# Attention's row maxima sent by GpSimd, score products emitted slot by slot, prologue loads sooner

## The chip, the cores and the metric

The program runs on one core of a Trainium2 chip. The number is the device time of one execution in microseconds (us): 728.79 us is the median of the kernel before, from two runs at 728.57 and 729.01 us. Engines are named as the profile names them: PE is TensorE (PEld its weight loads, PEq its sequencer), DVE is VectorE, ACT is ScalarE, POOL is GpSimd, SP is SyncE. [...]

## The reference

Two independent parts are computed and laid side by side in the last axis.

```python
# A: attention with memory.  S=2048, D=576, 32 heads of 18 channels, 4 segments of L=512
q,k,v = heads(x@wq), heads(x@wk), heads(x@wv)      # (1, 32, 4, 512, 18) each
M = 0; z = 0
for s in range(4):
    p = softmax(q[s] @ k[s].T * 18**-0.5 + causal_mask)     # 512 x 512 per head
    a_dot = p @ v[s]
    a_mem = (phi(q[s]) @ M) / (phi(q[s]) @ z + 1e-6)
    outs[s] = g*a_mem + (1-g)*a_dot                          # g = sigmoid(beta)
    M += phi(k[s]).T @ v[s];  z += sum(phi(k[s]))
a = concat(outs) @ wo
# B: spectral filter
b = irfft2(rfft2(x_B) * (w_r + 1j*w_i))
```

The softmax takes off the largest score of each row before the exponential. It is these row maxima that the change is about.

## The kernel before

**The stages.** By the profiled execution the forward transform of B takes the first 65 us. From there to about 265 us the projections of A run (q, k, v and the products for M). The inverse transform of B, sixteen steps `u` that PE bounds, lies between 280 and 349 us, and the prologue of the attention is laid between its steps. Attention runs from 351 to 682 us, and the last segment's output projection ends the program at 724 us. The text below is on the attention and its prologue.

**Stacks and row halves.** The 32 heads of 4 segments are 128 units of work, grouped in 16 stacks `n` of eight heads of one segment. A stack of Q (`s.Qs[n%3]`) and one of K (`s.Ks[n%4]`) stand in SBUF with four heads on partitions 0 to 63 (row half R=0) and four on partitions 64 to 127 (R=1). In each half 54 rows hold a head's 18 channels in bf16 parts. Q's rows 54 and 55 hold the row maxima in two bf16 parts, and K's same rows hold -1, so that a product over 56 rows is a score less its row's maximum. The first Q and K stack lie with the mask in one tile named `x0`, which the profile prints as `x`; the others are printed as `Qs` and `Ks`. A Q or K stack is loaded by four DMAs of `stack_dmas`, two of 384 KB and two small ones, which SP issues.

**One unit k.** There are 32 units `k`, two to a stack (`n,qd=divmod(k,2)`). For each, in this order:

1. `fill` (L689): products of 54 rows with one half's heads into a PSUM tile `s1`, of which there are three; then DVE takes the largest of each row into `mg` (L693). There are ten fills to a unit, of the kinds A, B and C, with sixteen reductions.
2. `mpath` (L701 to L710): POOL splits `mg` into two bf16 parts, `mh` (L701, L702); PE transposes them into PSUM, `mt` (L705); ACT copies that into SBUF, `mts` (L708); and two DMAs of 4 KB (`send`, L710) carry `mts` into rows 54 and 55 of the two halves of Q.
3. `s2` (L720 through `scores`): ten score tiles of 512 columns, each as a first pass (b=0, 56 rows, with the maxima) and a second pass (b=1, 54 rows) over a PSUM tile `s2`, of which there are four; then ACT takes the exponential into `P` (L729).
4. POOL puts zeros above the diagonal (`sel`, L743), four selects to a unit, two at once and two (`rest`) one step later.
5. `pv` (L766) multiplies P with V, ACT copies the result to `U` (L772), and DMAs carry U away.

**What sets the order.** `attention` is a loop of 133 steps `t`, with k=t//4 and hh=t%4. Each engine runs its instructions in the order in which it gets them. A step pops loads off the list `q` onto SP (three at t%8==0, else one), then emits `seg(t)`, a quarter of unit k's `s2` with fills of unit k+2 or k+3 between them, then background work, a part of `pv` of unit k-1, a part of `mpath`, and `rest`; last come the calls that `later` put off (`due`). `later(2,...)` runs a call two steps on. A fill, and so the maximum, of a unit is ready some steps ahead of its `s2`:

- hh=2 of unit k: `mpath(k+2)` starts on POOL;
- hh=3 of unit k: `mt` on PE, `mts` on ACT;
- hh=0 of unit k+1: the send, behind the step's two exponentials on ACT;
- hh=0 of unit k+2: the first `s2` that needs the rows.

The four loads of each of the stacks Qs(n+2) and Ks(n+3) come off the list from t%8==0 on.

**The prologue.** Units 0 and 1 and a part of unit 2 get their fills while the inverse runs: 15 steps with one or two fills each, two of 21 load calls popped in each step. The inverse yields several times for each `u`; one prologue step is taken at every fourth yield (`i%4==1`) beyond the seventh, and what is left is emitted behind the inverse. Here `send` goes to POOL (`s.now<0`), 4 DMAs in all; the other 60 go to ACT.

Of the kernel before, what the change touches and what calls it, by code (L numbers as in the profile page):

```python
# [6 lines left out]
AF=mybir.ActivationFunctionType; OP=mybir.AluOpType  # L7
# [95 lines left out]
class FFT:  # L103
# [4 lines left out]
    def forward(s,xp,cp,pp,wl,xs,consts):  # L108
# [301 lines left out]
class ATT:  # L410
# [284 lines left out]
    def mpath(s,k):  # L695

        nc=s.nc; n,qd=divmod(k,2); Q=s.Qs[n%3]
        mh=s.mh.rearrange("p a m -> p (a m)"); mg=s.mg.pop(k).rearrange("p (r h) i -> p r (h i)",r=2)
        hi,lo=[mh[:,:32].rearrange("p (r a m) -> p r a m",r=2,a=2)[:,:,a] for a in range(2)]
        e=nc.vector if s.now>=115 else nc.gpsimd  # L700
        e.tensor_copy(hi,mg)  # L701
        e.tensor_tensor(lo,mg,hi,op=OP.subtract)  # L702
        yield
        pt=s.psm.tile([128,1024],BF,name="mt",tag=s.mtag)[:,:128]
        nc.tensor.transpose(pt,mh,s.idb)  # L705
        yield
        mt=s.sm.tile([32,128],BF,name="mts",bufs=2)
        nc.scalar.copy(mt,pt[:32])  # L708
        def send(eng):
            for R in range(2): eng.dma_start(Q[64*R+54:64*R+56,0,2*qd:2*qd+2].rearrange("p h (i c) -> p (h i) c",c=128),mt[16*R:16*R+16])  # L710
        if s.now<0: send(nc.gpsimd)
        else: s.later(2,lambda: send(nc.scalar))
        yield
    def scores(s,p,n,J):

        Q,K=s.Qs[n%3],s.Ks[n%4]; f=True
        for b,rows in ((0,56),(1,54)):
            for i,(o,h,kb,qo) in enumerate(J):
                R,j=h//4,h%4; r=slice(64*R,64*R+rows)
                s.nc.tensor.matmul(p[:,o:o+512-qo],K[r,1-b,j,128*kb:128*kb+128],Q[r,b,j,qo:],start=f,stop=b==1,skip_group_check=True)  # L720
                f=False
    def s2(s,k,kind,x):
        nc=s.nc; n,qd=divmod(k,2); h=2*qd+(4*x if kind==2 else 4*(x//2)+x%2); tp=s.tp
        if k not in s.P: s.P[k]=[tp.tile([128,4,w],F32,name=f"P{i}") for i,w in enumerate((512,512,256))]
        P=s.P[k]
        p=s.ps.tile([128,512],F32,name="s2",tag="s2")
        J={0:[(0,h,0,0)],1:[(0,h,1,128),(384,h,3,384)],2:[(0,h,2,256),(256,h+1,2,256)]}[kind]
        s.scores(p,n,J)
        nc.scalar.activation(P[2][:,2*x:2*x+2].rearrange("p h c -> p (h c)") if kind==2 else P[kind][:,x],p,AF.Exp,scale=SC)  # L729
    def seg(s,t):  # L730

        k,q=divmod(t,4)
        L=(((0,0),("C",3),(0,2),("A",1)),((1,0),(1,2),("C",1),(2,1),("B",1),("B",0)),
           ((0,1),("A",2),(0,3),("C",0)),((1,1),(1,3),("A",3),(2,0),("C",2),("A",0)))[q]
        for a,x in L:
            if a in (0,1,2):
                if k<32: s.s2(k,a,x)
            elif k+2+q//2<32: s.fill(k+2+q//2,a,x)
        if k>31 or q%2==0: return
        P=s.P[k]  # L740
        def sel(x,a=0,b=1):
            x=x[:,a::b]
            s.nc.gpsimd.affine_select(out=x,in_=x,pattern=[[0,4//b],[1,128]],compare_op=OP.is_ge,fill=0.0,base=0,channel_multiplier=-1)  # L743
# [212 lines left out]
    def prologue(s):  # L956

        nc,io=s.nc,s.io
        yield
        s.load_v(0)  # L960
        q=s.stack_dmas(1,0)+s.stack_dmas(1,1)+s.stack_dmas(2,0)+s.stack_dmas(2,1)+[lambda: s.load_v(1)]+s.stack_dmas(3,1)
        for i in range(2): yield
        i=0; m=None
        O=((("C",3),("A",1)),(("C",1),("B",1)),(("B",0),)); E=((("A",2),("C",0)),(("A",3),("A",0)),(("C",2),))
        for k,F in ((0,E),(0,O),(1,E),(1,O),(2,E)):
            for f in F:
                for a,x in f: s.fill(k,a,x)
# [147 lines left out]
def emit(nc,tc,io):  # L1115
    def pool(es,name,bufs=1,**kw):
        return es.enter_context(tc.tile_pool(name=name,bufs=bufs,reuse_waits="tile",**kw))
    with ExitStack() as L0:
        cp=pool(L0,"cp"); dp=pool(L0,"dp",space=bass.MemoryType.DRAM)
        A=ATT(nc,tc,io,cp,dp)  # L1120
        Rz=ExitStack(); Rv=ExitStack(); Rw=ExitStack(); Ri=ExitStack(); L1x=ExitStack()
        tc.swap_default_side()
        zp=pool(Rz,"z"); ftp=pool(Rz,"ft")
        wq=pool(Rw,"wq")
        tc.swap_default_side()
        A.wh,A.wl={},{}
        F=FFT(nc,tc,io,zp); F.tp=A.ftp=ftp
        with tc.manual_schedule():
            x0=pool(L1x,"x0")
            with ExitStack() as es:  # L1130
                xp=pool(es,"xf",2); cf=pool(es,"cf"); st=pool(es,"st",2)
                pf=es.enter_context(PP(tc,"pf",dict(f1=2,c1=2)))
                F.forward(xp,cf,pf,A.load_w("wqk",1152,wq,st,576,"wst",4,1),A.first(Slots(x0),xp),A.consts)
            with ExitStack() as es:
                wv=pool(Rv,"wv"); xp=pool(es,"xp"); tp=pool(es,"tp",2); fwp=pool(es,"fw",2)
                pp=es.enter_context(PP(tc,"pp",dict(pj=5,pt=1,pm=2)))
                F.pace.add(F.middle(fwp)); F.pace.add(F.last())
                def hook(g,i):
# [12 lines left out]
                q0=[]  # L1151
                A.projections(xp,tp,pp,wv,F.pace,hook)
            Rv.close()
            with ExitStack() as L1:
                cp2=pool(L1,"cp2"); sm=pool(L1,"sm",2); sp=pool(L1,"sp",3)
                ps1=L1.enter_context(PP(tc,"ps1",dict(s1=3)))
                A.begin(sm,sp,ps1)
                with ExitStack() as es:
                    pi=es.enter_context(PP(tc,"pi",dict(i2=2,i3=2,mt=1)))
                    yl=pool(es,"yl",2)  # L1160
                    A.att_setup(cp2)
                    A.psm,A.mtag=pi,"mt"
# [27 lines left out]
```

## Time and profile before

| | us |
|---|---|
| median of 2 runs | 728.79 (728.57 to 729.01) |
| the profiled execution | 725.92 |
| its span | 724.2 |
| PE busy | 682.5 (94% of the span) |
| PE weight loads | 490.1 (68%) |
| DVE busy | 543.0 (75%) |
| ACT busy | 432.7 (60%) |
| POOL busy | 191.2 (26%) |
| mean granted PE clock | 0.978 of full speed |

The span is the time from the first to the last recorded instruction, and the execution is 1.7 us longer. "Busy" leaves out the time in which an engine issues DMAs. In a row of a timeline stand the start, the time that one takes, the engine, the line, the operation, out<-in, the shape, and in brackets how long the engine had stood idle and whom it waited for. In a row of waits stand the idle time, the number of waits and the longest or mean of them. A row of a table by windows has the length of the window, the busy time and number of instructions of PE, PEld, DVE, ACT and POOL, the granted clock, the share of the 16 DMA engines, and GB/s. In the DMA view, q1 is the queue of what SP issues, q10 that of ACT, and q0 that of POOL: packets, MB, and the share of the 16 engines' time.

### The profile page before, as it was taken

Reading aid. Unit: us, or ns where it says so; the run is one execution under the profiler, and the core shown is the slowest. Engines: PE = TensorE matmul, PEld = TensorE weight load, DVE = VectorE, ACT = ScalarE, POOL = GpSimd, SP = SyncE. Lnnn points to the kernel's source line nnn. Section 1 sums busy time; section 2 is a strip of 40 time slices with the busy share of each in tenths; the row PEclk is TensorE's granted clock in tenths of the full one; section 3 lists DMA queues with packets and bytes.
Section 4 is the critical chain, followed back from the end, with each engine's and each line's share of the span. In section 5 each row is a group of like instructions: output and inputs, shape, how many; then the busy total and the mean of one; then the engine's idle time right before and its main releaser. Section 6 shows DMA issues by size and latency. Waiting matters only on the chain.

```text
span 724.2 us, 15284 instructions
## 1 busy us (share of the span) xinstructions
PE 682.5 (94%) x5288; PEld 490.1 (68%) x5288; DVE 543.0 (75%) x1514; ACT 432.7 (60%) x900; POOL 191.2 (26%) x389
## 2 busy tenths in 40 slices
PE   9999999999999999999888798879999999899997
PEld 6999789789789799999534344434566445563496
DVE  5998988888898786777876776768656877468633
ACT  4876783873782844443476656648656676466421
POOL 2112000100100114572253322334323463133300
PEclk9999999999999999999898989999999999999999
DMA  9995665783685796998378865766766786333052
GB/s 344 301 286 140 191 184 161 249 267 107 208 264 135 220 287 185 247 248 193 108 147 166 173 142 118 187 164 130 163 122 172 188 173 132 77 118 92 24 168 71
DMA packets 79748, 127.66 MB, mean 176 GB/s; under 512 B 13052, under 2 KB 44442, under 8 KB 79542
## 3 DMA queue, kind: packets, MB, share of 16 engines
q1 hardware_dynamic: 72766, 110.67, 58.3%
q0 software_dynamic: 5824, 15.76, 8.0%
q8 instruction: 42, 0.69, 0.4%
q10 hardware_dynamic: 1080, 0.25, 0.2%
q14 instruction: 36, 0.29, 0.1%
HBM read 81.78 MB, written 43.92 MB: 174 GB/s over the span
## 4 chain that ended last, share of the span: by engine, by line
PE 50%; DMA 13%; DVE 7%; ACT 6%; issue 5%; POOL 2%; SPq 1%; ACTq 1%; DVEq 0%; POOLq 0%
PE pj L487 10%; PE pv L766 7%; DMA Qs<-mts 6%; PE pjv L487 6%; PE s L720 6%; PE i L331 4%; PE i L320 4%; DVE junk L693 4%; PE po L912 4%; PE s L689 3%; ACT P L729 2%; DMA x<-mts 2%; PE po L942 2%; PE pm L559 2%; DMA vD<-vt 1%
## 5 line engine op out<-in xcount | busy, mean ns | idle before, releaser
L693 DVE CUSTOM_DVE_ANT_0 junk<-s,x 128x384 bf16<-128x384 f32 (+3 forms) x512 | 218.4, 487 | 84.3 <-PE s L720 55.8
L729 ACT ACTIVATE P<-s 128x512 f32<-128x512 f32 x320 | 168.0, 605 | 54.9 <-PE s L720 33.0
L743 POOL TENSOR_SCALAR_AFFINE_SELECT P<-P 128x512 f32<-128x512 f32 (+1 forms) x131 | 78.9, 626 | 51.0 <-ACT P L729 50.3
L720 PEld LDWEIGHTS <-Ks 56*128 56x128 bf16 (+1 forms) x768 | 48.3, 96 | 52.6 <-issue 25.0
L766 PE MATMUL pv<-P,vs 128*32 128x512 f32 (+3 forms) x1024 | 81.9, 452 | 0.0
L720 PE MATMUL s<-Qs,Ks 56*128 56x512 bf16 (+7 forms) x512 | 66.9, 307 | 9.7 <-DMA Qs<-mts 7.1
L689 PE MATMUL s<-Ks,Qs 54*128 54x384 bf16 (+3 forms) x256 | 58.2, 309 | 5.1 <-DVE mg L693 5.1
L766 PEld LDWEIGHTS pv<-P,vs 128*32 128x32 f32 x1024 | 28.7, 112 | 50.1 <-issue 41.1
L487 PE MATMUL pj<-x,wqkh 128*128 128x512 f32 x162 | 56.1, 408 | 0.0
L232 DVE TENSOR_TENSOR Z<-Z 128x580 f32<-128x580 f32 (+2 forms) x51 | 45.9, 913 | 0.6
L693 DVE DVE_READ_ACCUMULATOR2_ANT mg<- 128x1 f32 x512 | 42.6, 83 | 0.0
L689 PEld LDWEIGHTS <-Qs 54*128 54x128 bf16 x320 | 27.2, 96 | 19.5 <-issue 13.6
L548 POOL MEMSET vt<- 128x32 f32 x16 | 2.4, 163 | 139.9 <-PE pm L559 121.6
L720 PE MATMUL s<-x,Ks 56*128 56x128 bf16 (+7 forms) x256 | 33.2, 305 | 5.3 <-DMA x<-mts 5.0
L320 PE MATMUL i<-civ,Y 128*128 128x256 f32 (+1 forms) x288 | 37.1, 282 | 0.9 <-POOL Y L305 0.9
L708 ACT COPY mts<-mt 32x128 bf16<-32x128 bf16 x32 | 8.1, 254 | 49.0 <-PE mt L705 47.3
L320 PEld LDWEIGHTS i<-civ,Y 128*128 128x128 f32 (+1 forms) x288 | 35.3, 180 | 1.3 <-POOL Y L305 1.3
L487 PE MATMUL pj<-x,wqkl 128*128 128x512 f32 x90 | 35.6, 395 | 0.0
L487 PE MATMUL pj<-xh,wqkh 128*128 128x512 f32 x90 | 35.5, 395 | 0.0
L487 PE MATMUL pj<-xh,wqkl 128*128 128x512 f32 x90 | 35.5, 395 | 0.0
L331 PE MATMUL i<-itab,T 128*128 128x290 f32 (+1 forms) x224 | 34.5, 304 | 0.6 <-ACT E L336 0.5
L506 DVE SCALAR_TENSOR_TENSOR ex<-pj,ex 128x512 f32<-128x512 f32 (+1 forms) x28 | 19.3, 690 | 20.7 <-ACT ex L504 20.7
(189 smaller groups left out, 1596.8 us busy)
## 6 DMA issues: line engine op xcount, KB each, us to landing
qkD<-sp SPq DMA_DIRECT2D x32, 384.0 KB
Ks<-qkD SPq DMA_DIRECT2D x24, 384.0 KB
x<-qkD SPq DMA_DIRECT2D x20, 384.0 KB
Qs<-qkD SPq DMA_DIRECT2D x20, 384.0 KB
xin<-xb SPq DMA_DIRECT2D x16, 384.0 KB
cfw<-cfw POOLq DMA_DIRECT2D x16, 384.0 KB, 4.5
civ<-civ POOLq DMA_DIRECT2D x16, 384.0 KB, 6.1
vs<-vD SPq DMA_DIRECT2D x16, 310.5 KB
```

The costliest lines, as they stand in the source:

```text
L232: s.nc.vector.tensor_tensor(o,a,b,op=op)
L320: nc.tensor.matmul(p[:m,k],Y[i][:,q,c*128:c*128+m],cc[:,hl,o:o+256],start=n==0,stop=n==5)
L331: nc.tensor.matmul(p,x,t,start=n==0,stop=n==6)
L487: s.nc.tensor.matmul(out,a,b,start=i==0,stop=i==len(L)-1)
L506: if r1>r0: nc.vector.scalar_tensor_tensor(e[r0:r1],ps[r0:r1],0.0,e[r0:r1],op0=OP.max,op1=OP.add)
L689: nc.tensor.matmul(p[:,o:o+128*i+128],Q[r,0,j,128*i:128*i+128],K[r,1,j,:128*(i+1)],start=True,stop=True)
L693: nc.vector.tensor_tensor_reduce(out=junk[:,:w],in0=p[:,o:o+w],in1=s.mask[:,512-w:],scale=1.0,scalar=-3.0e38, op0=OP.add,op1=OP.max,accum_ ...
L720: s.nc.tensor.matmul(p[:,o:o+512-qo],K[r,1-b,j,128*kb:128*kb+128],Q[r,b,j,qo:],start=f,stop=b==1,skip_group_check=True)
L729: nc.scalar.activation(P[2][:,2*x:2*x+2].rearrange("p h c -> p (h c)") if kind==2 else P[kind][:,x],p,AF.Exp,scale=SC)
L743: s.nc.gpsimd.affine_select(out=x,in_=x,pattern=[[0,4//b],[1,128]],compare_op=OP.is_ge,fill=0.0,base=0,channel_multiplier=-1)
L766: nc.tensor.matmul(s.pvt[32*hh:32*hh+32,128*j:],vt[:,152*j+19*h:152*j+19*h+32],mv[0][:,hh,mv[1]],start=j==0,stop=j>1,skip_group_check=True)
L912: nc.tensor.matmul(ps,a[t][:r,c],b[:r,t,w],start=i==0,stop=i==13)
```

## The change

It has three parts.

1. **The sends.** `send` now goes to POOL in the attention too, and with `later(0)` in place of `later(2)`: in the step of the copy `mts`, not two calls of `due` on. Sixty DMAs move from ACT's queue to POOL's.
2. **The order of the products.** `seg` before emitted a flat list of score tiles and fills. Now each step has two lists, one for each row half, and `s2` is a generator that yields behind each pass. One slot takes one pass or one fill from each list.
3. **The prologue.** Each prologue step pops three load calls, with a yield behind each, and the inverse takes a step at three of four yields (`i%4!=3`).

```diff
@@ mpath
-        def send(eng):
-            for R in range(2): eng.dma_start(Q[64*R+54:64*R+56,0,2*qd:2*qd+2].rearrange("p h (i c) -> p (h i) c",c=128),mt[16*R:16*R+16])
-        if s.now<0: send(nc.gpsimd)
-        else: s.later(2,lambda: send(nc.scalar))
+        def send():
+            for R in range(2): nc.gpsimd.dma_start(Q[64*R+54:64*R+56,0,2*qd:2*qd+2].rearrange("p h (i c) -> p (h i) c",c=128),mt[16*R:16*R+16])
+        if s.now<0: send()
+        else: s.later(0,send)
         yield
-    def scores(s,p,n,J):
-
-        Q,K=s.Qs[n%3],s.Ks[n%4]; f=True
-        for b,rows in ((0,56),(1,54)):
-            for i,(o,h,kb,qo) in enumerate(J):
-                R,j=h//4,h%4; r=slice(64*R,64*R+rows)
-                s.nc.tensor.matmul(p[:,o:o+512-qo],K[r,1-b,j,128*kb:128*kb+128],Q[r,b,j,qo:],start=f,stop=b==1,skip_group_check=True)
-                f=False
     def s2(s,k,kind,x):
...
-        s.scores(p,n,J)
-        nc.scalar.activation(P[2][:,2*x:2*x+2].rearrange("p h c -> p (h c)") if kind==2 else P[kind][:,x],p,AF.Exp,scale=SC)
-    def seg(s,t):
-
-        k,q=divmod(t,4)
-        L=(((0,0),("C",3),(0,2),("A",1)),((1,0),(1,2),("C",1),(2,1),("B",1),("B",0)),
-           ((0,1),("A",2),(0,3),("C",0)),((1,1),(1,3),("A",3),(2,0),("C",2),("A",0)))[q]
+        for b,rows in ((0,56),(1,54)):
+            for i,(o,h,kb,qo) in enumerate(J):
+                R,j=h//4,h%4; r=slice(64*R,64*R+rows)
+                nc.tensor.matmul(p[:,o:o+512-qo],K[r,1-b,j,128*kb:128*kb+128],Q[r,b,j,qo:],start=b==0 and i==0,stop=b==1,skip_group_check=True)
+            if b: nc.scalar.activation(P[2][:,2*x:2*x+2].rearrange("p h c -> p (h c)") if kind==2 else P[kind][:,x],p,AF.Exp,scale=SC)
+            yield
+    def half(s,k,q,L):
+
         for a,x in L:
             if a in (0,1,2):
-                if k<32: s.s2(k,a,x)
-            elif k+2+q//2<32: s.fill(k+2+q//2,a,x)
+                if k<32: yield from s.s2(k,a,x)
+            elif k+2+q//2<32:
+                s.fill(k+2+q//2,a,x)
+                yield
+    def seg(s,t):
+
+        k,q=divmod(t,4)
+        L=((((0,0),("A",1)),(("C",3),(0,2))),(((1,0),("C",1),("B",0)),((1,2),(2,1),("B",1))),
+           (((0,1),("C",0)),(("A",2),(0,3))),(((1,1),(2,0),("A",0)),((1,3),("A",3),("C",2))))[q]
+        for _ in itertools.zip_longest(*[s.half(k,q,l) for l in L]): pass
@@ prologue
                 for a,x in f: s.fill(k,a,x)
-                for _ in range(2):
-                    if q: q.pop(0)()
...
-                yield
+                for _ in range(3):
+                    if q: q.pop(0)()
+                    yield
@@ emit
-                        if i>7 and i%4==1: next(pr,None)
+                        if i>7 and i%4!=3: next(pr,None)
```

The three parts show in the order of the instructions. On ACT, before, at the end of unit 7 and the start of unit 8 (P_5525 and P_5526 are P tiles of unit 8, `Qs_3169` the Q stack into which unit 9's maxima go):

```order
L708 COPY mts<-mt 32x128
L772 COPY U<-pv 128x512
L729 ACTIVATE P_5525<-s_5528 128x512
L729 ACTIVATE P_5525<-s_5536 128x512
L710 DMA Qs_3169<-mts 2x8x128 x2
L729 ACTIVATE P_5526<-s_5552 128x512
```

The sends stand two exponentials behind their copy; in the order of after ACT has no L710 row in the attention. On POOL at the same place, first before, then after (P_5368 to P_5370 are unit 7's P tiles before, P_5370 to P_5372 after; the L701 row is the first of a unit's `mpath`):

```order
L702 TENSOR_TENSOR mh<-mg,mh 128x2x8
L743 AFFINE_SELECT P_5368<-P_5368 128x4x128
L743 AFFINE_SELECT P_5369<-P_5369 128x4x128 x2
L743 AFFINE_SELECT P_5370<-P_5370 128x4x128
L701 CAST mh<-mg 128x2x8
```

```order
L702 TENSOR_TENSOR mh<-mg,mh 128x2x8
L745 AFFINE_SELECT P_5370<-P_5370 128x4x128
L745 AFFINE_SELECT P_5371<-P_5371 128x4x128
L710 DMA Qs_3169<-mts 2x8x128 x2
L745 AFFINE_SELECT P_5371<-P_5371 128x4x128
L745 AFFINE_SELECT P_5372<-P_5372 128x4x128
L701 CAST mh<-mg 128x2x8
```

The sends now stand between a unit's second and third select, so the third and fourth select wait for `mts`, too. On PE, the start of unit 8's first step, first before, then after (s_5528 and s_5536 before, s_5530 and s_5538 after, are its score tiles; s_5532 and s_5540 are fills of unit 10):

```order
L705 MATMUL mt<-idb,mh 128x128
L720 LDWEIGHTS x_2634
L720 MATMUL s_5528<-Qs_3169,x_2634 128x512
L720 LDWEIGHTS x_2634
L720 MATMUL s_5528<-Qs_3169,x_2634 128x512
L689 LDWEIGHTS Qs_3170
L689 MATMUL s_5532<-Ks_3171,Qs_3170 128x512
```

```order
L705 MATMUL mt<-idb,mh 128x128
L724 LDWEIGHTS x_2634
L724 MATMUL s_5530<-Qs_3169,x_2634 128x512
L689 LDWEIGHTS Qs_3170
L689 MATMUL s_5532<-Ks_3171,Qs_3170 128x512
L724 LDWEIGHTS x_2634
L724 MATMUL s_5530<-Qs_3169,x_2634 128x512
```

The fill of the other half now stands between the two passes of the first score tile. On PE at the end of the inverse (L331 is its last product), first before, then after:

```order
L331 MATMUL i_4229<-itab_2955,T_4129 128x290
L689 LDWEIGHTS Qs_3169
L689 MATMUL s_4244<-Ks_3171,Qs_3169 128x384
L689 LDWEIGHTS Qs_3169
L689 MATMUL s_4244<-Ks_3171,Qs_3169 128x128
L689 LDWEIGHTS Qs_3169
L689 MATMUL s_4251<-Ks_3171,Qs_3169 128x512
L705 LDWEIGHTS mh
L705 MATMUL mt<-idb,mh 128x128
```

```order
L331 MATMUL i_4261<-itab_2955,T_4150 128x290
L689 LDWEIGHTS Qs_3169
L689 MATMUL s_4275<-Ks_3171,Qs_3169 128x512
L724 LDWEIGHTS x_2634
L724 MATMUL s_4302<-x_2634 128x512
```

Before, eight fill products, of which the first three are shown, and the transpose of unit 1 stand between the inverse and the first score product; after, one fill product does.

More of the change, by code (lines that the diff above doesn't have):

```diff
@@ L708, in mpath @@
         nc.scalar.copy(mt,pt[:32])
-        def send(eng):
-            for R in range(2): eng.dma_start(Q[64*R+54:64*R+56,0,2*qd:2*qd+2].rearrange("p h (i c) -> p (h i) c",c=128),mt[16*R:16*R+16])
-        if s.now<0: send(nc.gpsimd)
-        else: s.later(2,lambda: send(nc.scalar))
+        def send():
+            for R in range(2): nc.gpsimd.dma_start(Q[64*R+54:64*R+56,0,2*qd:2*qd+2].rearrange("p h (i c) -> p (h i) c",c=128),mt[16*R:16*R+16])
+        if s.now<0: send()
+        else: s.later(0,send)
         yield
-    def scores(s,p,n,J):
-        Q,K=s.Qs[n%3],s.Ks[n%4]; f=True
-        for b,rows in ((0,56),(1,54)):
-            for i,(o,h,kb,qo) in enumerate(J):
-                R,j=h//4,h%4; r=slice(64*R,64*R+rows)
-                s.nc.tensor.matmul(p[:,o:o+512-qo],K[r,1-b,j,128*kb:128*kb+128],Q[r,b,j,qo:],start=f,stop=b==1,skip_group_check=True)
-                f=False
     def s2(s,k,kind,x):
         nc=s.nc; n,qd=divmod(k,2); h=2*qd+(4*x if kind==2 else 4*(x//2)+x%2); tp=s.tp
+        Q,K=s.Qs[n%3],s.Ks[n%4]
         if k not in s.P: s.P[k]=[tp.tile([128,4,w],F32,name=f"P{i}") for i,w in enumerate((512,512,256))]
@@ L727, in s2 @@
         J={0:[(0,h,0,0)],1:[(0,h,1,128),(384,h,3,384)],2:[(0,h,2,256),(256,h+1,2,256)]}[kind]
-        s.scores(p,n,J)
-        nc.scalar.activation(P[2][:,2*x:2*x+2].rearrange("p h c -> p (h c)") if kind==2 else P[kind][:,x],p,AF.Exp,scale=SC)
+        for b,rows in ((0,56),(1,54)):
[5 more added lines that the diff above has]
+    def half(s,k,q,L):
+        for a,x in L:
+            if a in (0,1,2):
+                if k<32: yield from s.s2(k,a,x)
+            elif k+2+q//2<32:
+                s.fill(k+2+q//2,a,x)
+                yield
     def seg(s,t):
         k,q=divmod(t,4)
-        L=(((0,0),("C",3),(0,2),("A",1)),((1,0),(1,2),("C",1),(2,1),("B",1),("B",0)),
-           ((0,1),("A",2),(0,3),("C",0)),((1,1),(1,3),("A",3),(2,0),("C",2),("A",0)))[q]
-        for a,x in L:
-            if a in (0,1,2):
-                if k<32: s.s2(k,a,x)
-            elif k+2+q//2<32: s.fill(k+2+q//2,a,x)
+        L=((((0,0),("A",1)),(("C",3),(0,2))),(((1,0),("C",1),("B",0)),((1,2),(2,1),("B",1))),
+           (((0,1),("C",0)),(("A",2),(0,3))),(((1,1),(2,0),("A",0)),((1,3),("A",3),("C",2))))[q]
+        for _ in itertools.zip_longest(*[s.half(k,q,l) for l in L]): pass
         if k>31 or q%2==0: return
```

## The prediction

> **What bounds the kernel now.** The page first. PE is busy for most of the span and leads the chain of work that ended last, but one DMA stands high in that chain:
>
> ```profile
> span 724.2 us, 15284 instructions
> PE 50%; DMA 13%; DVE 7%; ACT 6%; issue 5%; POOL 2%; SPq 1%; ACTq 1%; DVEq 0%; POOLq 0%
> PE pj L487 10%; PE pv L766 7%; DMA Qs<-mts 6%; PE pjv L487 6%; PE s L720 6%; PE i L331 4%; PE i L320 4%; DVE junk L693 4%; PE po L912 4%; PE s L689 3%; ACT P L729 2%; DMA x<-mts 2%; PE po L942 2%; PE pm L559 2%; DMA vD<-vt 1%
> ```
>
> `Qs<-mts` (6%) and `x<-mts` (2%) are the 4 KB sends. Who waits for them is told by the view of the tile mts over the whole program, and where, by PE's waits from 358 to 474 us:
>
> ```profile
>   PE s L720: 14.3, 6
> PE s L720 <- DMA Qs<-mts: 9.3, 4, 2.4
> PE s L720 <- DMA x<-mts: 5.0, 2, 3.3
> ```
>
> Score products stood still six times for 14.3 us, all in that stretch (9.3 + 5.0). One of them in the timeline, from the copy to the product that waits:
>
> ```profile
> 425.48 1.81 POOL L743 TENSOR_SCALAR_AFFINE_SELECT P<-P 128x512 f32<-128x512 f32 x3 [0.34 <-ACT P L729]
> 426.71 0.26 ACT L708 COPY mts<-mt 32x128 bf16<-32x128 bf16 x1 [0.81 <-PE mt L705]
> 427.53 0.65 ACTq L710 DMA_DIRECT2D Qs<-mts  x1
> 428.22 0.62 ACTq L710 DMA_DIRECT2D Qs<-mts  x1
> 432.77 1.28 PE L766 MATMUL pv<-P,vs 128*32 128x384 f32 x16
> 436.39 0.60 PE L720 MATMUL s<-Qs,x 56*128 56x512 bf16 x1 [2.17 <-DMA Qs<-mts]
> ```
>
> The copy is done at 426.97, ACT issues 0.56 us later, and 8 us on PE still has no maxima. The DMA view of the two stretches says why (queue, packets, MB, share of the 16 engines' time; 427.5 to 434.8 us first, then 434.8 to 436):
>
> ```profile
> q1 hardware_dynamic: 354, 1.21, 96.6%
> ...
> q1 hardware_dynamic: 74, 0.17, 68.3%
> q10 hardware_dynamic: 36, 0.01, 7.2%
> ```
>
> ACT's queue q10 moved no packet for 7.3 us while SP's stack loads filled q1; its 36 packets (two sends) ran when SP's were through. What a stall costs beyond its idle time is seen in windows (length; PE, PEld, DVE, ACT, POOL busy; clock, DMA share, GB/s), and in the `U` copies, one to a unit:
>
> ```profile
> 358.00:474.00 116.00, 98.03 (x989) 46.23 (x990) 86.62 (x401) 76.33 (x158) 44.53 (x86) 0.91 0.72 150
> 426.00:434.00 8.00, 7.76 (x94) 3.57 (x86) 7.21 (x35) 5.83 (x12) 3.32 (x8) 1.00 0.99 184
> 560.00:580.00 20.00, 19.18 (x182) 8.92 (x182) 16.30 (x67) 14.53 (x32) 9.55 (x15) 1.00 0.73 176
> 366.99 0.57 ACT L772 COPY U<-pv 128x512 f32<-128x512 f32 x1
> ...
> 426.87 0.57 ACT L772 COPY U<-pv 128x512 f32<-128x512 f32 x1
> 434.42 0.57 ACT L772 COPY U<-pv 128x512 f32<-128x512 f32 x1
> 446.50 0.57 ACT L772 COPY U<-pv 128x512 f32<-128x512 f32 x1
> ...
> 465.23 0.57 ACT L772 COPY U<-pv 128x512 f32<-128x512 f32 x1
> ```
>
> From 366.99 to 465.23 lie ten units in 98.24 us. A unit without a stall takes 7.55 us (434.42 - 426.87), one with a stall 12.08 (446.50 - 434.42). The granted clock is 1.00 in the undisturbed windows and 0.91 over the stretch: 9% of 116 us is 10.4 us of full-speed clock not granted, behind the stalls.
>
> **The change part by part: the sends.** Ten clean units would take 75.5 us, so the stretch holds 98.24 - 75.5 = 22.7 us. An estimated 2 of these are work that only this stretch has (the memory part starts in it), which leaves 20.7 as the most that can go. The least, if the sends come in time, is the idle time itself, 14.3. I take 19, near the upper end, since a product at half clock costs time as surely as a wait does.
>
> Do they come in time? POOL's sends have a row only in the prologue, the first answer here for 349 to 357 us and the second for 325 to 330, with a window beside them:
>
> ```profile
> L710 POOL DMA_DIRECT2D x<-mts x2: 566/568/571, 349.7 to 350.2; - x2
> DMA to landing us min/median/max: 3.9/4.0/4.1
> DMA to landing us min/median/max: 6.5/6.9/7.2
> 350.00:354.00 4.00, 3.51 (x21) 1.88 (x21) 3.86 (x17) 1.40 (x3) 1.33 (x3) 0.61 0.78 215
> ```
>
> The first pair ran beside SP's loads, at a DMA share of 0.78, and landed 4 us after its issue; the second pair stood behind a 384 KB table load in POOL's own queue, which attention hasn't. The need: the next clean unit would begin at about 434.2 (436.39 - 2.17). The sends are issued behind the copy at 426.97 and 427.54, so the later lands at 431.6 by the first row and at 434.7 by the second. At a share of 0.99 I take 4.5 us, 432.0, with 2.2 us to spare. By the second row a stall of 0.5 us is left in each of six places, with its clock: some 6 of the 19 us.
>
> The Trainium skill, page "DMA: Bandwidth & Descriptors", section "Issuing engines are not separate DMA queues", speaks against this part: DMAs of all issuing engines run on the same 16 engines and interleave, and several issuers save only the sequencer's issue time; by it the sum would have no 19 in it. The row of q10 doesn't bear out the interleaving for ACT behind SP, and 4.0 us beside a loaded q1 speaks for POOL, though at 0.78.
>
> On POOL, 60 sends of 0.57 us are 34 us more. They are covered: it is busy 44.5 of the 116 us. But they stand ahead of a unit's third and fourth select and wait for the copy. In the rows above the four selects are over at 427.29 (425.48 + 1.81) and the pv that reads the last ones starts at 432.77: 5.5 us to spare. Issued after 426.97, the sends take until 428.1, and two selects of 0.6 us follow until 429.3, so 3.4 us are left. Cost 0; were that cover gone, each us beyond it would cost up to 30 us in all.
>
> On ACT 60 issues of 0.62 us, 37 us, go. ACT is busy 76.3 of the 116 us, so this is worth nothing by itself, but for one place where the issue waited:
>
> ```profile
> 620.23 3.44 ACTq L710 DMA_DIRECT2D Qs<-mts  x2
> 623.78 1.09 ACT L729 ACTIVATE P<-s 128x512 f32<-128x512 f32 x2 [4.09 <-DMA Qs<-mts]
> 624.43 0.37 PE L720 MATMUL s<-Qs,Ks 56*128 56x512 bf16 x1 [2.00 <-ACT P L729]
> ```
>
> Two issues took 3.44 us where two at 0.62 take 1.24, the exponentials behind them came late, and PE stood for 2.0 us. That goes: -2.0 (0 if it stands for another reason).
>
> **The slots.** They change which half's product stands next. Before, a fill of the other half stands behind both passes of a score tile. PE's rows at one such place:
>
> ```profile
> 576.26 0.39 PE L720 MATMUL s<-Qs,Ks 56*128 56x512 bf16 x1
> 576.27 0.39 PE L689 MATMUL s<-x 54*128 54x512 bf16 x1
> 576.49 0.38 PE L720 MATMUL s<-Qs,Ks 54*128 54x512 bf16 x2
> L689 PE MATMUL s<-Ks,Qs 54*128 54x384 bf16 (+3 forms) x256 | 58.2, 309 | 5.1 <-DVE mg L693 5.1
> L693 DVE CUSTOM_DVE_ANT_0 junk<-s,x 128x384 bf16<-128x384 f32 (+3 forms) x512 | 218.4, 487 | 84.3 <-PE s L720 55.8
> ```
>
> The fill starts 0.01 us behind the first pass and 0.22 ahead of the second: the halves run side by side already. What does hold a fill is a free `s1` tile, so DVE (5.1 us in the program), whose reductions alone take 218.4/32 = 6.8 us of a unit's 7.55. A slot order can take those 5.1 us away or, with fills earlier, double them: -5.1 to +5.1, and I take 0, since DVE's pace isn't changed.
>
> **The prologue.** At the end of the inverse:
>
> ```profile
> 348.53 0.39 PE L689 MATMUL s<-Ks,Qs 54*128 54x384 bf16 x3
> 349.01 0.39 PE L689 MATMUL s<-Ks,Qs 54*128 54x384 bf16 x2
> 350.25 0.38 PE L689 MATMUL s<-Ks,Qs 54*128 54x384 bf16 x2 [0.85 <-DVE mg L693]
> 350.87 1.03 PE L720 MATMUL s<-x 56*128 56x512 bf16 x2
> ```
>
> From 348.53 to 350.87 are 2.34 us, of which 0.85 are a wait for DVE. Seven of eight fill products move in among the inverse's products, where they cost PE their streaming. Between 0.85 and 2.34 I take -1.5. The loads, a third call per step, go sooner past the inverse's own traffic; that costs nothing while all are in by the step that asserts them.
>
> **The sum.** 19 + 2.0 + 0 + 1.5 = 22.5 off 725.92 is 703.4. The profiled execution is 2.9 us under the median of 728.79, so 706 for the median.
>
> **The rivals.** (1) *POOL's sends land no sooner than ACT's.* Under a share of 0.99 they wait for SP's loads until about 435, as ACT's do. For it: q10's silence; against it: the 4.0 us above. The stalls stay and 2.0 + 1.5 go: 725. Chance 0.13.
>
> (2) *Another wait takes the place.* The stack loads themselves move 0.72 x 116 = 84 us of full DMA in a stretch that shrinks to 97, and one more transfer waits in it already (PE's waits, 474 to 490 us):
>
> ```profile
> PE pb L844 <- DMA rd<-rdD: 3.0, 1, 3.0
> ```
>
> If loads or that chain of round trips are late by what the units gain, half of the 19 comes back: 716. Against it: the window 426 to 434, at 0.99, ran at full pace. Chance 0.15.
>
> (3) *The slots count after all.* Were PE to start products strictly in order, then neighbours of different halves alone would overlap. Counting so, the four steps of a unit took 4 + 6 + 4 + 6 slots and now 3 + 5 + 3 + 5. Four slots of 0.23 us (576.49 - 576.26) in 32 units are 29 us: 677. Against it stands the start of 576.27. Chance 0.04. The Trainium skill, "TensorE: Matmul & The Clock Gate", section "Part 3: Packing small matmuls — row/col tiling", has such a rule (matmuls start and end strictly first in, first out); the trace has the fill out ahead of a pass that was emitted before it.
>
> (4) *Slower: POOL holds the selects.* If the two sends occupy POOL for over 3.4 us beyond the 1.1 above, as ACT's pair did once for 2.2 us beyond its own, pv comes late in each unit. At 1.5 us over the cover, 30 units lose 45 us: 751. It decides from 3.4 us; against it, the prologue's sends at 0.57 us each. Chance 0.05.
>
> **How the numbers follow.** The forecast has the remaining 0.63. Its own range: 19 becomes 14.3 or 20.7 and slots ±5.1, so 699 to 716. The range of 8 in 10 takes in rival 2 and most of rival 1: 699 to 725. A measurement of this kernel tells about 2% (14.6 us) from no change, so faster is below 714.2 and slower above 743.4. Faster: 0.63, less 0.02 of its upper end, with rival 3 and 0.06 of rival 2, 0.71. Slower: rival 4, 0.05. Within 2%: the other 0.24.
>
> **What would show it.** Right: no row of PE waiting for `mts` between 358 and 474 us, `U` copies 7.5 to 8 us apart there, a clock near 1.0 in that window, POOL's L710 landing in 4 to 5 us with q0 packets while q1 is over 90%, and PE's score segments as long as before in clean units. Wrong: landings of 7 us (rival 1), another releaser of L720 or the `pb` wait above 3 us (2), shorter units at 560 to 580 us (3), or pv waiting for POOL (4).

## The result and the profile after

The changed kernel's median is 718.09 us (717.79 and 718.39) against 728.79 before: a ratio of 0.985, 95% interval 0.981 to 0.990. The forecast was 706, a gain of 22.8 us, and 10.7 were measured: right in sign, inside the range, and under half of the size. Beside the experiments the same kernel was timed twice more on other chips, at 712.24 us (ratio 0.978, 0.974 to 0.983) and 717.93 us (0.987, 0.982 to 0.993). Its executions there lie between 704 and 721 us, and why they spread so is a part of what follows. Some executions are marked slow because they took over 1.5% longer than the fastest of their kernel (among them two of e3's six and nine of e10's twelve), and while the medians below are of all executions, the ratios leave these out.

The profile after is of the execution at 717.79 us. First come PE's waits from 358 to 474 us, then the wait for the tile mts in the whole program, then the window of that stretch:

```profile
PE s L724 <- DMA Qs<-mts: 10.6, 4, 3.4
PE s L724 <- DMA x<-mts: 3.5, 2, 2.7
PE s L689 <- DVE mg L693: 1.9, 4, 1.1
```

```profile
  PE s L724: 14.9, 8
```

```profile
358.00:474.00 116.00, 99.19 (x975) 45.01 (x974) 83.78 (x388) 73.89 (x154) 55.72 (x105) 0.85 0.75 152
```

The stalls on the maxima are all there: 14.1 us in the stretch where they were 14.3, and 14.9 in all, and the granted clock there fell from 0.91 to 0.85. The `U` copies show where the 8.1 us of span came from:

```profile
363.53 0.57 ACT L774 COPY U<-pv 128x512 f32<-128x512 f32 x1
...
419.45 0.58 ACT L774 COPY U<-pv 128x512 f32<-128x512 f32 x1
426.54 0.57 ACT L774 COPY U<-pv 128x512 f32<-128x512 f32 x1
442.01 0.58 ACT L774 COPY U<-pv 128x512 f32<-128x512 f32 x1
...
462.47 0.58 ACT L774 COPY U<-pv 128x512 f32<-128x512 f32 x1
...
647.66 0.57 ACT L774 COPY U<-pv 128x512 f32<-128x512 f32 x1
```

There is one copy to a unit, and ten units lie between the first and the eleventh. The first copy is 3.46 us sooner (366.99 - 363.53). The ten units of the stretch take 98.94 us where they took 98.24. From there to the copy at 647.66 (655.72 before) the changed kernel wins 5.3, and nothing behind it. So in this execution nothing came from the stretch on which 19 of the forecast's 22.5 us stood. Within it a clean unit is shorter, 7.09 us (426.54 - 419.45) in place of 7.55, and a unit with a stall longer, 15.47 at the place above.

One send in the timeline (the q of SPq marks SP's own instruction queue, which issues DMAs), and the DMA queues while it is under way (window 420 to 426 us), with its landing by the view of the tile:

```profile
417.44 0.78 SPq L668 DMA_DIRECT2D x<-qkD  x2
418.98 0.78 SPq L668 DMA_DIRECT2D Ks<-qkD  x2
419.29 0.26 ACT L708 COPY mts<-mt 32x128 bf16<-32x128 bf16 x1 [0.57 <-PE mt L705]
419.85 1.13 POOL L710 DMA_DIRECT2D Qs<-mts  x2 [0.92 <-ACT mts L708]
429.38 0.61 PE L724 MATMUL s<-Qs,x 56*128 56x512 bf16 x1 [3.04 <-DMA Qs<-mts]
```

```profile
q1 hardware_dynamic: 323, 1.11, 102.6%
```

```profile
DMA to landing us min/median/max: 9.5/9.5/9.6
```

POOL issues 0.3 us behind the copy, as the diff says. But SP's four 384 KB loads were issued from 2.4 us ahead of the send on, POOL's q0 moved no packet in the six us shown, and the send landed 9.5 us after its issue. ACT's queue had done no worse before: issued at 427.53, its packets ran at about 435.

### The profile page after: what moved, and what is told of

It is laid out like the page before. It is cut to its first block, busy times and chain, and to the rows that moved or that the text cites. A ratio compares the mean times of both kernels' runs of the same rounds, so it can differ in the third digit from the quotient of the medians.

```text
span 716.1 us, 15314 instructions
## 1 busy us (share of the span) xinstructions
PE 677.5 (95%) x5288; PEld 483.7 (68%) x5288; DVE 542.9 (76%) x1514; ACT 432.4 (60%) x900; POOL 225.8 (32%) x449
## 5 line engine op out<-in xcount | busy, mean ns | idle before, releaser
L768 PE MATMUL pv<-P,vs 128*32 128x512 f32 (+3 forms) x1024 | 86.1, 471 | 0.0
L724 PE MATMUL s<-Qs,Ks 56*128 56x512 bf16 (+7 forms) x512 | 65.4, 311 | 8.1 <-DMA Qs<-mts 7.6
L689 PE MATMUL s<-Ks,Qs 54*128 54x128 bf16 (+3 forms) x256 | 56.8, 305 | 5.9 <-DVE mg L693 4.7
L710 POOL DMA_DIRECT2D Qs<-mts x40 | 22.7, 569 | 46.2 <-ACT mts L708 46.2
L724 PE MATMUL s<-x,Ks 56*128 56x512 bf16 (+7 forms) x256 | 32.8, 308 | 4.0 <-DMA x<-mts 3.5
L331 PE MATMUL i<-itab,T 128*128 128x290 f32 (+1 forms) x224 | 36.4, 304 | 0.2 <-DVE yout L339 0.2
```

What stands on the lines that cost most here:

```text
L331: nc.tensor.matmul(p,x,t,start=n==0,stop=n==6)
L689: nc.tensor.matmul(p[:,o:o+128*i+128],Q[r,0,j,128*i:128*i+128],K[r,1,j,:128*(i+1)],start=True,stop=True)
L710: for R in range(2): nc.gpsimd.dma_start(Q[64*R+54:64*R+56,0,2*qd:2*qd+2].rearrange("p h (i c) -> p (h i) c",c=128),mt[16*R:16*R+16])
L768: nc.tensor.matmul(s.pvt[32*hh:32*hh+32,128*j:],vt[:,152*j+19*h:152*j+19*h+32],mv[0][:,hh,mv[1]],start=j==0,stop=j>1,skip_group_check=True)
```

## The experiments

Each kernel is the one named with the edit shown. The experiments ran on five chips, and each ratio is to runs of the kernel before on the same chip.

### The three parts alone

e1 is the kernel before with part 1 of the change, e2 with part 2, e3 with part 3, and e4 has parts 2 and 3 with the sends as before (`s.later(2,lambda: send(nc.scalar))`).

> The kernel before with part 1 alone (sends on POOL, in the step of the copy). The forecast of the prediction: sends land in 4 to 5 us, the six stalls go, 707 to 709 us. Theory A (a send waits for SP's stack loads whichever engine issues it; the gain came from parts 2 and 3): landings of 6 to 10 us for odd units, six or so stalls of 1.8 to 3.4 us between 358 and 474 us stay, 724 to 729 us. Theory B (the POOL path itself is what is slow): the same time, so this run doesn't tell A from B.

> The kernel before with part 2 alone (slot by slot). The prediction: no change, 723 to 734. Theory A: a clean unit early in attention takes 7.1 us in place of 7.55 (as in the trace of the changed kernel) and later ones 0.2 us less, about 25 units, so 5 us less or a little more: 721 to 725; the stalls stay and may grow by what the units gain.

> The kernel before with part 3 alone (prologue sooner). The prediction: -1.5 us, 727. By the trace of the changed kernel, whose first unit ends 3.5 us sooner and which has no stretch of half clock at 351 us: -3 to -3.5, so 725 to 726, if nothing later takes it back.

> The changed kernel with the sends as before (ACT, later(2)). The prediction: 727, since all but 1.5 us were to come from the sends. Theory A: as fast as the changed kernel but for the one lane wait of ACT, 716 to 721, with stalls of the same number and size; a rival, that free ACT time makes the units shorter (7.55 to 7.08), gives 724 to 726.

| kernel | median us | ratio to before (95%) |
|---|---|---|
| e1, sends | 715.80 | 0.985 (0.980 to 0.989) |
| e2, slots | 726.66 | 1.001 (0.999 to 1.004) |
| e3, prologue | 719.84 | 0.990 (0.985 to 0.994) |
| e4, slots and prologue | 724.02 | 0.999 (0.996 to 1.001) |
| before | 727.33 | |

Theory A, that the sends gave nothing, falls: they alone give as much as the whole change. But they give 11 us and not 19, between the two times expected, and the parts don't add. e1's trace shows stalls that are shorter, not gone (PE's waits, 358 to 474 us, then one stall, then a window across it):

```profile
PE s L720 <- DMA Qs<-mts: 6.2, 5, 2.2
PE s L720 <- DMA x<-mts: 2.2, 2, 1.1
```

```profile
393.74 0.39 PE L720 MATMUL s<-Qs,Ks 56*128 56x512 bf16 x1 [1.29 <-DMA Qs<-mts]
```

```profile
376.00:396.00 20.00, 17.19 (x191) 8.54 (x187) 15.53 (x75) 15.05 (x32) 13.08 (x22) 1.00 0.83 169
```

The window 376 to 396 holds two stalls of 1.05 and 1.29 us and its clock stays at 1.00. In the kernel before, each of the places with a stall of 2.2 us or more has a clock of 0.62 to 0.83 in the 7 to 10 us around it. e2 shows where the slots' gain goes: a clean unit takes 7.1 us as in the changed kernel, but its ten units take 97.72 us beside 98.24, so other units lose what a clean one wins (PE's waits, 350 to 650 us):

```profile
PE s L724 <- DMA Qs<-mts: 11.6, 7, 3.8
PE s L724 <- ACT P L725: 7.4, 9, 2.6
```

The 2.4 us for ACT of the kernel before are 7.4 here, the longest stall on maxima is 3.8 us where it was 3.3, though their sum fell from 14.3 to 11.6, and the clock from 358 to 474 us is 0.85 where it was 0.91. e3's median is 8 us lower, but its times spread from 713 to 728 us and its trace is of an execution at 727.50, so that trace (first copy 1.6 us sooner) can't show where the gain lies. e4, with slots added, has lost most of it.

### The time of the send, or its engine

```diff
 e5  -  s.later(0,send)    +  s.later(0,lambda: send(nc.scalar))
 e13 -  s.later(0,send)    +  s.later(2,send)
```

Both are the changed kernel with one edit: ACT sends in the step of the copy, or POOL sends where ACT did before.

> The changed kernel itself, beside the others on one chip. If the parts simply add, it equals the sum of parts 1 to 3 as measured alone (about -13 for the sends, -8 for the prologue, 0 for the slots): 705. If the slots take back what the sends give (a unit that is done sooner only waits longer for maxima that land when SP's loads are through): 716 to 720, as its first two runs.

> The changed kernel with its sends issued by ACT, in the same step as POOL's now are (right behind the copy). Theory A (any queue's small DMA waits until SP's loads are through): landings of 6 to 9 us for odd units, stalls of 1.8 to 3.4 us, 716 to 724. Theory B (the software path of POOL is what is slow, early hardware sends would come in time): landings of 2 to 3 us, no stalls, 698 to 708.

> The changed kernel with POOL's sends at the place that ACT's had (later(2), behind the next step's work). This parts the engine from the time of the send. If the time is what counts (ahead of or behind SP's loads): the sends are issued 0.3 to 2 us later, more stalls, 718 to 726. If the engine counts (ACT's exponentials no longer stand behind a send): the same as the changed kernel, 708 to 716.

Measured: the changed kernel 712.24 us, between its two expectations; e5 726.28 (0.999, 0.995 to 1.003); e13, on another chip, 731.39 (1.009, 1.005 to 1.013). So the time of the send counts, and POOL with ACT's time is even slower than before and than was expected, with stalls on `Qs<-mts` that rose from 10.9 us to 22.6 (350 to 650 us, e13):

```profile
PE s L724 <- DMA Qs<-mts: 22.6, 8, 5.7
```

e5 missed both of its numbers, since a third thing happened. ACT's sends came nearly in time, but ACT had them ahead of exponentials for which PE then waited (358 to 474 us, e5):

```profile
PE s L724 <- ACT P L725: 15.5, 11, 4.3
PE s L724 <- DMA Qs<-mts: 1.6, 1, 1.6
```

e5's ten units take 87.93 us, 10.3 less than before, so the early sends did pay in the stretch. Behind it, with 11.8 us more of such waits up to 690 us, e5 takes 203.0 us to the last copy on ACT where the kernel before takes 190.5. This is what POOL is good for: with the sends on POOL in the same step, these waits are 0.5 us in the changed kernel's first trace.

The profile of the changed kernel on that chip (span 702.4 us) shows both cases in one run. An odd unit (the second of its stack) at 414 us:

```profile
414.06 0.26 ACT L708 COPY mts<-mt 32x128 bf16<-32x128 bf16 x1 [0.57 <-PE mt L705]
414.61 1.14 POOL L710 DMA_DIRECT2D Qs<-mts  x2 [0.91 <-ACT mts L708]
415.61 0.80 SPq L668 DMA_DIRECT2D x<-qkD  x2
```

```profile
DMA to landing us min/median/max: 2.9/3.6/4.4
```

Here SP was later with its loads, the send went 1.0 us ahead of them, and it landed in 2.9 and 4.4 us, as the prediction had it. In the first profile it went 2.4 us behind them and took 9.5. The ten units of this execution take 85.12 us (364.58 to 449.70) and PE's stalls on maxima from 358 to 474 us are 5.8: here the stretch gave 13.1 us.

The three traces of the changed kernel hold more sends to go by. Counted by how many of SP's 384 KB loads (L668) were issued in the nine us ahead of a send:

| loads ahead | sends | landing, us (median) |
|---|---|---|
| none | 50 | 1.7 to 5.5 (2.8) |
| one or two | 81 | 2.1 to 8.4 |
| three or four | 49 | 6.0 to 10.6 (8.5) |

Who is first is decided within two or three us. A stall may help the loads, since SP goes on while PE stands, and so keep an execution in one case; that would explain executions that differ by up to 17 us, but it was not tested by itself.

### Without the loads

e8 is the changed kernel in which the two 384 KB loads of each stack are left out from stack n=4 on, so that it works on old rows there.

```diff
-            L.append(lambda R=R,m=m: nc.sync.dma_start(flat(T[64*R:64*R+48]),m))
+            if n<4: L.append(lambda R=R,m=m: nc.sync.dma_start(flat(T[64*R:64*R+48]),m))
+            else: L.append(lambda: None)
```

> The changed kernel without the two 384 KB loads of each stack from the fourth on (their stacks hold old rows; all else is computed as before). Theory A (SP's loads hold the sends and, as rows queued ahead of it, the small load ry that DVE waits for): every send of POOL lands in 2 to 4 us, no stall on maxima over 1 us between 380 and 474 us, 690 to 700. Theory B (POOL's sends are slow in themselves): stalls stay, 710 or more.

Measured: 693.26 us. Its window of the stretch and the landings from 380 to 440 us:

```profile
358.00:474.00 116.00, 109.50 (x1175) 50.42 (x1175) 102.75 (x474) 90.30 (x189) 70.21 (x128) 0.97 0.37 99
```

```profile
DMA to landing us min/median/max: 1.8/2.4/3.9
```

No stall on maxima is left, and the ten units take 72.67 us (364.24 to 436.91). The loads hold the sends; POOL's path by itself takes 2.4 us.

### The sends ahead of the loads

Two ways were tried. e6 issues the sends on SP's own queue, in program order ahead of the loads; e7 does so for odd units and leaves the even ones on POOL.

```diff
 e6  +  s.later(0,lambda: send(nc.sync))
 e7  +  s.later(0,lambda: send(nc.sync if k%2 else nc.gpsimd))
```

> The changed kernel with its sends issued by SP, in program order ahead of the loads of the next stacks, which then start behind the copy of the maxima. Theory A: the odd units' sends land in 2 to 3 us since nothing is ahead of them in q1, the loads start 1 to 2 us later, most of the stalls on maxima between 358 and 474 us go with their half clock, 698 to 708; the even units' sends stand behind the rest of the loads and must be in by the next unit but one. Theory B (a send is slow in itself, 5 us or more): stalls stay, 715 or more. Rival C: the loads, later now, are the next wait (PE waiting for fills of the unit after next): 710 to 718.

> As the run before, but only the odd units' sends are issued by SP (those that collide with the start of a burst of loads); the even units' stay with POOL. Theory A: 698 to 708, with no stall on maxima left but what even units have; rival C: 710 to 718.

Measured: 712.93 us (0.978, 0.973 to 0.983) and 712.91 (0.978, 0.974 to 0.981), beside 712.24 for the changed kernel: rival C. Stalls on maxima fall to 4 to 5 us, but the small load `ry` now comes late, and DVE's reductions are queued behind it. PE's waits in e6, and DVE's row:

```profile
PE s L689 <- DVE mg L693: 9.2, 10, 6.1
PE s L724 <- DMA Qs<-mts: 3.9, 3, 1.9
445.18 0.95 DVE L793 RECIPROCAL ry<-ry 128x128 f32<-128x128 f32 x1 [6.04 <-DMA ry<-rD]
```

Without the loads (e8) PE's longest wait for DVE in the stretch is 1.1 us, so it is the loads that hold `ry`, too.

The other way is to make the maxima sooner. e14 emits the transpose, the copy and the send ahead of the step's `pv`; e15 emits them behind the third of the five slots of that step, with the send ahead of the selects.

```diff
 e14 (attention)
+            if hh==3 and m is not None: steps(m,2)
             if 4<=t-1<132: s.pv((t-5)//4,(t-5)%4)
-            if hh==3 and m is not None: steps(m,2)
 e15 (seg; s.hook is steps(m,2) where hh==3; send() in place of later(0,send))
-        for _ in itertools.zip_longest(*[s.half(k,q,l) for l in L]): pass
+        for i,_ in enumerate(itertools.zip_longest(*[s.half(k,q,l) for l in L])):
+            if q==3 and i==2 and s.hook: s.hook(); s.hook=None
```

> The changed kernel beside the next three on one chip: 710 to 719.

> The changed kernel with the transpose, the copy and the send of the maxima emitted ahead of the step's pv (before: behind it). By the trace of the changed kernel that gives the copy 0.6 to 1.1 us sooner. If the order of the send and of SP's next loads decides (a send ahead of them lands in 3.5 to 5.5 us, one 2 us behind them in 9 to 11): fewer stalls, 703 to 711. If SP's loads start sooner by the same, or it isn't enough: 711 to 717.

> The same, sooner still: the transpose stands behind three of the five slots of that step's products, and the sends stand on POOL ahead of the step's selects. Copy and send come about 1.5 us sooner than in the changed kernel, ahead of the last score products on which SP's loads wait. If the order decides: most odd units' sends land in 4 to 6 us, no or one stall on maxima, 697 to 707. If PE now waits for POOL's mh, or the selects stand behind the sends and hold pv: 712 or more, with those waits in the profile.

| kernel | median us | ratio to before (95%) |
|---|---|---|
| the changed kernel | 717.93 | 0.987 (0.982 to 0.993) |
| e14 | 709.94 | 0.977 (0.973 to 0.980) |
| e15 | 717.43 | 0.987 (0.984 to 0.990) |

e14 does what was expected where the order decides: its stalls on maxima from 358 to 474 us are 8.9 us, beside 14.3 in the trace of the changed kernel on that chip. e15's time says nothing until its trace is read by stages. Its `U` copies:

```profile
365.25 0.58 ACT L774 COPY U<-pv 128x512 f32<-128x512 f32 x1 [0.51 <-PE pv L768]
...
447.89 0.59 ACT L774 COPY U<-pv 128x512 f32<-128x512 f32 x1 [0.51 <-PE pv L768]
```

The ten units take 82.64 us, against 98.24 before and 98.94 in the changed kernel. That is 15.6 us off, and one stop of DVE stands in it still. PE's waits from 350 to 690 us and that stop tell where it went:

```profile
PE s L689 <- DVE mg L693: 9.1, 11, 5.4
PE mt L705 <- POOL mh L702: 7.9, 6, 2.3
PE pb L846 <- DMA rd<-rdD: 3.4, 1, 3.4
PE mt L705 <- DVE mh L702: 2.4, 1, 2.4
PE s L723 <- DMA Qs<-mts: 1.8, 3, 1.0
```

```profile
438.64 0.95 DVE L793 RECIPROCAL ry<-ry 128x128 f32<-128x128 f32 x1 [5.39 <-DMA ry<-rD]
```

1.8 us for `Qs<-mts` are left of 10.9 in the changed kernel. In their place come DVE's stand at `ry` (5.39 us) and, all but 0.3 us of them behind 474 us, PE's own waits for `mh` (7.9 and 2.4), which the early transpose brings in. From the eleventh copy (447.89) to the last on ACT (644.79) e15 takes 196.9 us, where the changed kernel takes 185.2 (462.47 to 647.66): there most of the gain went.

### The second wait

e10 puts the reciprocal and what follows it two steps later for both chains that use it (`rr`, the row sums, and `rd`, the memory part), e16 for `rr` alone.

```diff
 e10 (recip)
+        if s.now<110:
+            yield
+            yield
 e16 (recip)
+        if not eps and s.now<110:
+            yield
+            yield
```

> The changed kernel with DVE's reciprocal of the row sums (and what follows it) two steps later, in all but the last segment, so that DVE doesn't stand with reductions queued behind it while the load ry waits behind SP's stack loads. If that wait has taken the place of the one on the maxima: the stops of PE for DVE at 441 and for rd at 469 us (2.7 and 3.6 us in a profile of the changed kernel) shrink to under 1, with 3 to 7 us of half clock: 702 to 708. If it hides nothing, the same as the changed kernel, 710 to 715.

> The changed kernel with the reciprocal of the row sums (rr) alone two steps later; the one of the memory part (rd), which had a stop of 7 us in the earlier run, stands as in the changed kernel. If DVE's stand at the ry load is the next wait: 2 to 5 us less than the changed kernel beside it; if what follows the reciprocal comes late instead, the same or slower.

e10: 723.60 us (ratio 0.988, 0.982 to 0.993, from three executions), slower than the changed kernel on any chip (712.24 to 718.09); `rd`, on which PE waits, came too late, 10.9 us in two waits:

```profile
PE pb L849 <- DMA rd<-rdD: 10.9, 2, 7.1
```

e16: 710.05 us (0.976, 0.971 to 0.980), 7.9 less than the changed kernel beside it, and more than expected. Its stalls on maxima stay (14.2 us), and so do its ten units (97.62 us). Its gain lies behind them: from the eleventh copy to the last one on ACT its trace takes 179.8 us (463.48 to 643.26), that of the changed kernel beside it 186.7 (462.79 to 649.53). So it isn't the same time as e14's.

### Both together, and the parts in e9

e9 has parts 1 and 3 without the slots. e18 is e14 with e16's edit. e17 has e15's early transpose and send up to step 43 alone, e14's place behind that, and e16's edit.

> The changed kernel without the slots (parts 1 and 3). If parts add as measured alone: 713.8 and 717.8 against 726.5, so 705. If slots take back what they give, by asking for the maxima 0.45 us sooner in each unit: this kernel is as fast as the changed one or faster, 704 to 712. If slots are worth their 0.45 us in each clean unit and 0.2 later: slower than the changed one by 4 or more, 716 or more.

> e14 (transpose ahead of pv) with the reciprocal rr two steps later. If the two gains (about 8 each against the changed kernel beside them) are of different waits and add: 700 to 704. If they are the same time taken twice: 708 to 711.

> The sends of e15 (transpose inside the step's products, send ahead of the selects) up to step 43 alone, where it cost nothing; behind that the place of e14; and the reciprocal rr two steps later as in e16. If the 17 us that e15 was ahead of the changed kernel at 433 us are the gain that the prediction counted, and the stop for DVE behind ry gave back the most: 696 to 704. If something else gives them back in the same stretch (rd, SP's loads of the memory part): 705 to 712.

| kernel | median us | ratio to before (95%) |
|---|---|---|
| e9 | 713.95 | 0.982 (0.978 to 0.986) |
| e18 | 709.94 | 0.977 (0.971 to 0.982) |
| e17 | 703.62 | 0.968 (0.963 to 0.974) |

e9 can't be told from the changed kernel (0.978 to 0.987), so it decides between none of its expectations. e18's two gains did not add: 709.94 is e14's time again, and its trace has 12.2 us of stalls on maxima where e14's had 8.9. e17 beats both kernels, by 25 us against the runs of before beside it (728.99). Its ten units:

```profile
365.36 0.58 ACT L775 COPY U<-pv 128x512 f32<-128x512 f32 x1 [0.51 <-PE pv L769]
...
445.17 0.58 ACT L775 COPY U<-pv 128x512 f32<-128x512 f32 x1 [1.38 <-PE pv L769]
```

79.81 us, 18.4 less than before. The stretch has a gain of that size in it, when the maxima come in time. Over the traces the ten units follow the stalls on maxima (PE's waits, 358 to 474 us):

| trace | execution, us | ten units, us | stalls on maxima, us |
|---|---|---|---|
| before | 725.92 | 98.24 | 14.3 |
| changed, three traces | 717.79, 718.10, 704.07 | 98.94, 97.95, 85.12 | 14.1, 14.3, 5.8 |
| e1 | 717.62 | 88.31 | 8.4 |
| e14 | 711.83 | 90.21 | 8.9 |
| e15 | 717.52 | 82.64 | 2.4 |
| e17 | 699.06 | 79.81 | 2.1 |
| e8, loads left out | 694.25 | 72.67 | none |

## Why the prediction was right and wrong

**What bounds the stretch: right.** Small sends behind SP's loads, 14.3 us of idle PE and its clock on top. Without the loads (e8) no such stall is left, and with the sends ahead of them (e17, which has e16's edit too) the ten units lose 18.4 us. Of those, ten units' shorter pace by the slots is 4.6 (10 x 0.46), so about 14 are the sends'. By the same count e8's 25.6 us less are 21. So what the stretch holds, 14.3 to 20.7, was sized rightly; 19 would have needed nearly all sends in time.

**"Do they come in time?": the step that failed.** The prediction took 4.5 us from issue to landing, from a row at 349.7 us (3.9 to 4.1 us at a DMA share of 0.78), and said that a share of 0.99 adds half a us. The changed kernel's trace has 9.5 us at 420. The share was the wrong measure: what counts is whether the loads were issued ahead of the send, and over three traces the sends with no load in the nine us ahead landed in 2.8 us (median), those with three or four in 8.5. The row at 349.7 us was of the favourable order: in that trace SP issued its next loads (`vs` and `wo`) at 349.92 and 350.45, its last 384 KB load had been at 335.45, and only a store of 290 KB (`yb`, 349.54) was just ahead. The trace of before also had the rows for the place itself, ahead of the copy's end at 426.97:

```profile
424.62 0.78 SPq L668 DMA_DIRECT2D x<-qkD  x2
426.16 0.78 SPq L668 DMA_DIRECT2D Ks<-qkD  x2
```

A send behind that copy stood behind 384 KB pieces in flight, whichever queue it took, and q10's silence fits that order. (The 36 packets of q10 ran beside 74 of q1, so SP's loads were not quite through, as the prediction has it.)

**Rival 1 (POOL's sends land no sooner), 0.13: that is what the first profile shows,** stalls of 14.9 us. Its price of 725 was 7 us too high, because two other terms were too small. The first copy came 3.46 us sooner in that trace, where 1.5 were counted, and the low clock at 351 us went (the window 350 to 354 had 0.61, now 1.00); in the other two traces it came 2.4 and 2.2 us sooner, and 1.6 with the prologue alone (e3). The stretch from 462 to 648 us gave 5.3, where 2.0 were counted for ACT's wait; in e9, without the slots, it takes 3.9 us longer than in the changed kernel, so by these two traces most of it is the slots'. That 718 lies inside the range of 699 to 725 is therefore luck: in that execution the gain came from terms that the sum had at 3.5 us, and none from the 19.

**The slots, 0: mis-sized.** A clean unit went from 7.55 to 7.09 us. The windows of one clean unit, before and then after:

```profile
426.87:434.42 7.55, 7.11 (x81) 3.38 (x77) 6.75 (x32) 5.84 (x13) 2.87 (x7) 1.00 1.00 176
```

```profile
419.45:426.54 7.09, 6.80 (x81) 3.20 (x77) 6.76 (x32) 5.77 (x14) 4.04 (x8) 1.00 1.03 190
```

DVE (the third busy time) does the same work, 6.75 and 6.76 us, in 7.55 and in 7.09, so the slots took out idle time of DVE that the prediction had not looked for, and 0.3 us of PE's busy time. That nothing changes because DVE's work is unchanged was wrong. But e2 at 1.001 and e9 beside the changed kernel show that a shorter clean unit gives the whole program little while the maxima wait for the loads; that it is paid back as a longer stall fits the 3.04 and 3.40 us in the first trace, but was not parted from the order of the sends. Rival 3 (29 us) did not come.

**Rival 2 (another wait takes the place): right of what comes next.** In e6, e7 and e15, where most maxima come in time, PE stops for DVE's stand at `ry` 3.3 to 6.1 us at a time and for `rd` 3.4 to 4.9. In e15 it was rather the new waits for `mh`, which its own edit made, that took back most of the gain. In the first trace of the changed kernel they were small (1.9 and 2.2 us), so this rival is not what made the forecast wrong.

**POOL's cover and rival 4:** right. Two issues take 1.13 us and no row of PE waits for POOL's selects. The long issue on ACT at 620 us is gone: the score products' waits for ACT from 350 to 650 us fell from 2.4 to 0.5 us.

What stays open: why e3 alone gives 8 us in the median, and why e16's delay gives 8, mostly behind the stretch, where PE's waits for DVE were small in the changed kernel beside it. Both may move later work against the loads, and no run here parts that from what they do directly. Why small transfers wait for the larger ones of another queue isn't shown either, only that they do.

## What to carry to other kernels

Where a small transfer on a critical path meets large ones, ask which is issued first, and not only how full the DMA engines are: read the issue times of both off one timeline, and move the small one's producer, not only its queue. A shorter stage ahead of such a wait may be worth nothing until the wait goes, as the slots alone were here (e2, 1.001). And judge a change by stages: e15 and the changed kernel have the same total, and one of them had the whole gain and lost it elsewhere.

## What the runs showed of the hardware

- POOL's queue, too, moved nothing while loads that SP had issued earlier ran: no q0 packet from 420 to 426 us at a q1 share of 102.6%, and 9.5 us to landing, against 2.4 us (median) with the loads left out. Over three traces of the changed kernel, sends with none of these loads in the nine us ahead landed in 1.7 to 5.5 us, those with three or four in 6.0 to 10.6.
- The length of a single stall of PE did not tell whether it cost clock. Two of 1.05 and 1.29 us, 16 us apart, left the granted clock at 1.00 (e1, 376 to 396 us), but two of 1.13 and 1.09 us, 1.7 us apart, gave 0.83 from 408 to 418. In the changed kernel's execution at 704 us, one of 2.08 us left 1.00 (370 to 385 us) and one of 1.73 gave 0.72 (388 to 394). The changed kernel's window behind its 3.04 us stall:

```profile
426.00:434.00 8.00, 4.96 (x34) 1.49 (x32) 2.00 (x10) 2.50 (x5) 2.38 (x5) 0.68 0.47 95
```
